# Which engine empties one transposed tile: two pairs of the first batch on VectorE instead of ScalarE, in a fused attention and MLP kernel

## The chip, the cores and the metric

The kernel runs on one core of a Trainium2 chip (trn2). The metric is the device time of one execution in microseconds, taken as the median over runs; the times quoted from a profile come from one profiled execution of the same program. Engines are named as in the profile: PE is TensorE (PEld its weight loads), DVE is VectorE, ACT is ScalarE, POOL is GpSimd, SP issues DMAs.

## What is computed

Inputs are fp32: four batches of eight heads, 576 positions, head size 64. Causal attention with a bias from a running sum is followed by two MLP blocks:

```python
scores = scale * np.matmul(q, k.transpose(0, 1, 3, 2))
cum = np.cumsum(np.maximum(s, 0.0), axis=-1)
bias = -(cum[:, :, :, None] - cum[:, :, None, :])
scores = np.where(causal, -1e9, scores + np.minimum(bias, 0.0))
attn = np.exp(scores - np.max(scores, axis=-1, keepdims=True))
attn = attn / (np.sum(attn, axis=-1, keepdims=True) + 1e-09)
x = np.matmul(attn, v)                       # heads side by side: 512 wide
h = gelu(x @ w_in); u, v = h[..., :512], h[..., 512:]
y = x + (u * (w_sg @ layernorm(v) + b_sg)) @ w_out
xk, xr = mixes of y and y shifted by one position
out = sigmoid(xr @ w_r) * (np.maximum(xk @ w_k, 0.0) ** 2 @ w_v)
```

## The kernel before

Each fp32 product is done as two or three products of parts: a value is cast to `F32R` (the high part) and the rest is kept as a low part (`split_lo`, L65). Weights of the first MLP come as 64-bit words and are put together by `convert` (L72 to L83): two ScalarE steps, two VectorE steps on `y` and `t` (L78, L80), a ScalarE cast (L83), a low part (L65).

`attn_pair` (L202 on) does two heads at a time. For each head, SP loads `kq`; the query half is cast into `qb` (L223, tile `QB`) and the key half into `ka` (L224); two DMAs (L225, L226) copy these parts to the other 64 partitions of `qa` and `ka`, and two splits on POOL (L65) write the low parts to `qa` and `kb` (tile `KB`). From the second batch on, and for most heads of the first, `QB` and `KB` are two fixed sets, used in turn, so the operands of a head can only be written when the head before the last is read for the last time. In the first batch heads go through three sets (`hd % 3`).

Nine score steps follow for a pair, by head and tile of 128 query rows: four of the first head, one (`2_4`) for the last 64 rows of both heads, four of the second head. A step multiplies the operands into a PSUM bank `sc` (L246, L247; two buffers), VectorE adds the mask and takes the row minimum of the negated scores (L271, `mx`), ScalarE takes the exponential (L279). Then PE transposes the tile in 128x128 blocks into a bank `tp` (L294, L297) and one copy takes the bank to SBUF: tile 1 to `pt1` by ScalarE (L299), tiles 2 and 3 to `pt2` (L301), the last 64 rows by two ScalarE copies and one of VectorE (L307, L308). Tile 3 is the one with four blocks, 128x512. In the first batch its copy was ScalarE's, in the others VectorE's. Its bank is one of the three `acc` banks in the first batch. In the end PE multiplies with the values (`pv`, L327) and the result, times the reciprocal sums, goes to `xT` (L340, L341).

`moe1(b)` is the first MLP of a batch: products `v` and `u` (L356) with evacuation by a gelu on ScalarE (L473), layer norm, `sg`, `o`. It is interleaved with the attention of the next batch. In the first batch all its PSUM banks are the three `acc` banks in turn. Its remaining weight pieces are loaded and converted on the way (`first_wc`, through three `tmp` buffers for `wr` and `wy`).

The program fixes the order in which instructions are created; a scheduler then sets the order on each engine from its own estimates of durations, so a changed engine for one copy can move instructions on all queues. Names in the order lists below carry a running number: `sc_2_4_1_782` is a score bank of step `2_4` (second chunk) of pair 3, and `tp_0_3_769` the transposes of tile 3 of the first head of pair 3. Pairs count from 0; pair 3 has heads 6 and 7, pair 4 heads 8 and 9.

Of the kernel before, what the change touches and what calls it, by code (L numbers as in the profile page):

```python
# [36 lines left out]
def fused_kernel(ctx, tc, kqT, vL, s, w_in, g_ln, w_sgT, b_sg, w_out, mu_k, mu_r, w_k, w_v, w_r, out):  # L37
    nc = tc.nc
# [163 lines left out]
    def attn_pair(b, hp):  # L202
        pr = b * (H // 2) + hp
        first = b == 0
        ops = []
        for hh in range(2):
# [5 lines left out]
            i = hd % (NSET + 1) if first else hd % NSET  # L212
# [31 lines left out]
        def scores(sc, hh, q, c0, c1, m):  # L244
            qa, ka, qb, kb = ops[hh]
            nc.tensor.matmul(sc[:m, :c1 - c0], qa[:, q], ka[:, c0:c1], start=True, stop=False)  # L246
            nc.tensor.matmul(sc[:m, :c1 - c0], qb[:, q], kb[:, c0:c1], start=False, stop=True)  # L247
# [3 lines left out]
        for hh, i in steps:  # L251
            q0 = i * P
            w = min(q0 + P, S)
            if first and hh != 1:
                st = stf[:, 64 * i * (i + 1):64 * (i + 1) * (i + 2)]
            else:
                st = at.tile([P, 640], F32, tag="st", name=f"st{pr}_{hh}_{i}", bufs=4)
            mx = at.tile([P, 2], F32, tag="mx", name=f"mx{pr}_{hh}_{i}", bufs=4)
            chunks = [(0, min(w, 512))] + ([(512, w)] if w > 512 else [])
            for ci, (c0, c1) in enumerate(chunks):  # L260
                sc = psum1.tile([P, 512], F32, tag="sc", name=f"sc{pr}_{hh}_{i}_{ci}", bufs=2)
                n = c1 - c0
                if hh < 2:
                    scores(sc, hh, slice(q0, w), c0, c1, P)
                    mk = mask[:, 512 - q0 + c0:512 - q0 + c0 + n]
                else:

                    scores(sc, 1, slice(w - P, w), c0, c1, P)
                    scores(sc, 0, slice(q0, w), c0, c1, 64)
                    mk = mask2 if ci else mask[:, :512]  # L270
                nc.vector.tensor_tensor_reduce(  # L271
                    out=st[:, c0:c1], in0=sc[:, :n], in1=mk, op0=ALU.add, op1=ALU.min,
                    scale=-SCALE, scalar=mx[:, 0:1] if ci else BIG, accum_out=mx[:, ci:ci + 1],
                )
            if hh == 2:

                nc.gpsimd.memset(st[:, w:w + 64], 0.0)
            last = len(chunks) - 1
            e = nc.scalar.activation(  # L279
                st[:, :w], st[:, :w], AF.Exp, bias=mx[:, last:last + 1], scale=-1.0,  # L280
                accum_out=sm[:, 4 * hh + i % 4:4 * hh + i % 4 + 1],
            )
            if gelus:
                after(e, gelus[-1])
            exps.append(e)
            yield 2 * w

            if i == 0:
                st0 = st
                continue  # L290
            tag = "acc" if first and i > 2 else "tp"
            tp = psum1.tile([P, 512], F32, tag=tag, name=f"tp{pr}_{hh}_{i}", bufs=3)
            if i == 1:
                nc.tensor.transpose(tp[:, 0:P], st0[:, 0:P], ident)  # L294
            for j in range(min(i + 1, 4)):
                c = (j + (i == 1)) * P
                nc.tensor.transpose(tp[:, c:c + P], st[:, j * P:(j + 1) * P], ident)  # L297
            if i == 1:
                nc.scalar.copy(pt1[:, hh], tp[:, :QS + P])  # L299
            elif i < 4:  # L300
                (nc.vector.tensor_copy if i == 3 and not first else nc.scalar.copy)(  # L301
                    pt2[:, hh, :i + 1, q0 - QS:w - QS], tp[:, :(i + 1) * P].rearrange("p (j m) -> p j m", m=P))
            else:
                tp4 = psum1.tile([P, 512], F32, tag="tp", name=f"tq{pr}", bufs=3)
                nc.tensor.transpose(tp4[:, 0:P], st[:, 512:640], ident)
                for a in range(2):
                    nc.scalar.copy(pt2[:, a, :4, q0 - QS:], tp.rearrange("p (j a m) -> p a j m", j=4, a=2)[:, a])  # L307
                nc.vector.tensor_copy(pt2[:, :, 3, 0:64], tp4[:, :P].rearrange("p (a m) -> p a m", a=2))  # L308
            yield (i + 1) * 200
# [6 lines left out]
        for r in range(2):  # L316
# [16 lines left out]
            for j in range(2):  # L333
                i = 2 * r + j
# [133 lines left out]
    def after(late, early):  # L468
        tc.add_manual_dep(late.ins, early.ins.name, mybir.DependencyInfo(mybir.DependencyClass.NoSync, mybir.DependencyReason.DATA),
                          reason="activation tables")  # L470
# [18 lines left out]


    pairs = [attn_pair(b, h) for b in range(B) for h in range(H // 2)]

    def a_stream():
# [173 lines left out]
```

## Time and profile before

| what | us |
|---|---|
| median of 3 runs | 719.56 (716.68 to 719.63) |
| profiled execution | 719.3 |
| its span, first to last instruction | 717.5 |
| PE busy | 675.9 (94%) |
| DVE busy | 405.7 (57%) |
| ACT busy | 386.6 (54%) |
| POOL busy | 243.5 (34%) |

The span is what the profile's instructions cover; the execution's own time is 1.8 us longer. Busy shares are means over stages: the first batch's attention fills about the first 85 us, attention and first MLP together go on to about 390, and the second MLP fills the rest.

### The profile page before, as it was taken

How to read it: one execution, taken by the hardware profiler on the slowest of the kernel's cores; microseconds unless marked ns; L12 is line 12 of the kernel's file. 1: busy time of each engine (PE TensorE's matmuls, PEld its weight loads, DVE VectorE, ACT ScalarE, POOL GpSimd, SP SyncE). 2: the span in 40 equal slices, each digit the busy share in tenths (PEclk: the TensorE clock that was granted, in tenths of full speed). 3: DMA queues.
4: the chain of work that ended last, by engine and by line, in shares of the span. 5: the costliest groups of instructions: out<-in, count | busy, mean ns of one | idle time of the engine just before them, and what ended most of it. 6: DMA issues, size and time to landing. Idle time of an engine off the chain costs nothing.

```text
span 717.5 us, 12717 instructions
## 1 busy us (share of the span) xinstructions
PE 675.9 (94%) x4720; PEld 604.8 (84%) x4720; DVE 405.7 (57%) x874; ACT 386.6 (54%) x878; POOL 243.5 (34%) x243
## 2 busy tenths in 40 slices
PE   2779988899999999999999989999999999999998
PEld 1456777787888878889878889899999999999997
DVE  7886586757663555672554579889535144413411
ACT  5777665856565565455564576689535144512400
POOL 7445544375352765253651120001502030330000
PEclk9979999999999999999999999999999999999999
DMA  7753533434533235524123763652310120000001
GB/s 214 211 192 106 148 99 122 139 112 131 160 114 118 70 84 164 163 66 152 35 54 92 242 209 119 179 167 93 107 43 6 62 67 1 17 25 27 1 18 48
DMA packets 33036, 74.95 MB, mean 104 GB/s; under 512 B 4368, under 2 KB 8464, under 8 KB 32976
## 3 DMA queue, kind: packets, MB, share of 16 engines
q1 hardware_dynamic: 32976, 74.15, 34.4%
q8 instruction: 37, 0.61, 0.4%
q14 instruction: 23, 0.19, 0.1%
HBM read 50.84 MB, written 13.79 MB: 90 GB/s over the span
## 4 chain that ended last, share of the span: by engine, by line
PE 80%; DVE 10%; DMA 4%; issue 3%; ACT 2%; POOL 0%; SPq 0%; DVEq 0%; ACTq 0%; POOLq 0%
PE vo L356 14%; PE k L356 14%; PE pv L327 8%; PE r L356 7%; PE o L356 6%; PE sg L356 6%; PE v L356 6%; PE u L356 5%; PE tp L297 4%; PE sc L246 4%; PE sc L247 3%; DMA wr<-in_w_out_dram 1%; DMA wc<-wscr 1%; DVE lt L559 1%; DVE QB L223 1%
## 5 line engine op out<-in xcount | busy, mean ns | idle before, releaser
L356 PE MATMUL k<-xvn,wk 128*128 128x288 f32 x768 | 102.9, 295 | 0.5 <-DVE y L460 0.5
L356 PEld LDWEIGHTS k<-xvn,wk 128*128 128x128 f32 x768 | 102.2, 188 | 0.8 <-DVE y L460 0.8
L279 ACT ACTIVATE st<-st,mx 128x128 f32<-128x128 f32 (+4 forms) x124 | 72.0, 582 | 43.1 <-DVE mx L271 42.7
L246 PE MATMUL sc<-ka,qa 128*128 128x512 f32 (+4 forms) x180 | 63.8, 360 | 23.0 <-DMA ka<-ka 11.6
L271 DVE CUSTOM_DVE_ANT_0 st<-sc,mask 128x512 f32<-128x512 f32 (+3 forms) x124 | 61.2, 504 | 25.6 <-PE sc L247 19.9
L327 PE MATMUL pv<-pt,vf 128*64 128x320 f32 (+4 forms) x448 | 66.9, 371 | 1.2 <-ACT u L473 1.0
L356 PE MATMUL sg<-wsg,vn 128*128 128x288 f32 x448 | 66.6, 299 | 0.1
L246 PEld LDWEIGHTS sc<-ka,qa 128*128 128x128 f32 (+1 forms) x180 | 33.3, 185 | 37.9 <-DVE mx L271 16.3
L356 PEld LDWEIGHTS sg<-wsg,vn 128*128 128x128 f32 x448 | 60.7, 188 | 2.2 <-issue 1.0
L65 POOL TENSOR_TENSOR KB<-kq,ka 64x576 fp32r<-64x576 f32 x29 | 43.3, 1493 | 51.1 <-ACT ka L224 34.7
L65 POOL TENSOR_TENSOR xvn<-lt,xvn 128x576 fp32r<-128x576 f32 x12 | 19.6, 1642 | 114.1 <-ACT xvn L560 74.3
L618 DVE SCALAR_TENSOR_TENSOR o<-vo,sg 128x288 f32<-128x288 f32 x32 | 14.5, 455 | 77.2 <-PE vo L356 77.1
L247 PE MATMUL sc<-KB,QB 128*128 128x512 f32 (+3 forms) x180 | 57.4, 334 | 0.6 <-DMA KB<-crt 0.6
L327 PEld LDWEIGHTS pv<-pt,vf 128*64 128x64 f32 x448 | 36.2, 138 | 25.6 <-issue 7.8
L356 PE MATMUL vo<-kh,wvb 128*128 128x288 f32 x256 | 56.5, 295 | 0.0
L356 PE MATMUL vo<-kh,wva 128*128 128x288 f32 x256 | 56.1, 295 | 0.0
L587 ACT ACTIVATE lk<-k 128x288 f32<-128x288 f32 x64 | 26.1, 408 | 50.4 <-PE k L356 46.2
L356 PE MATMUL r<-xxs,wr 128*128 128x288 f32 x384 | 53.2, 295 | 0.0
L356 PEld LDWEIGHTS r<-xxs,wr 128*128 128x128 f32 x384 | 51.7, 188 | 0.0
L297 PE MATMUL tp<-ident,st 128*128 128x128 f32 x300 | 49.0, 281 | 2.5 <-ACT st L279 2.5
L356 PE MATMUL v<-wv,xs 128*128 128x512 f32 x192 | 50.4, 401 | 0.7 <-ACT v L473 0.5
L65 POOL TENSOR_TENSOR qa<-kq,QB 64x576 fp32r<-64x576 f32 x29 | 43.9, 1512 | 16.5 <-DVE QB L223 6.1
(166 smaller groups left out, 1521.2 us busy)
## 6 DMA issues: line engine op xcount, KB each, us to landing
wc<-wscr SPq DMA_DIRECT2D x24, 512.0 KB
kq<-in_kqT_dram SPq DMA_DIRECT2D x32, 288.0 KB
vf<-in_vL_dram SPq DMA_DIRECT2D x16, 320.0 KB
ydram<-y SPq DMA_DIRECT2D x16, 288.5 KB
yt<-ydram SPq DMA_DIRECT2D x16, 288.5 KB
out_dram<-o SPq DMA_DIRECT2D x16, 288.0 KB
qa<-QB SPq DMA_DIRECT2D x30, 144.0 KB
ka<-ka SPq DMA_DIRECT2D x30, 144.0 KB
```

The costliest lines, as they stand in the source:

```text
L65: eng.tensor_tensor(out=lo, in0=x, in1=f32(hi), op=ALU.subtract)
L223: (nc.scalar.copy if hd < 2 else nc.vector.tensor_copy)(qb[64:128], kq[64:128])
L246: nc.tensor.matmul(sc[:m, :c1 - c0], qa[:, q], ka[:, c0:c1], start=True, stop=False)
L247: nc.tensor.matmul(sc[:m, :c1 - c0], qb[:, q], kb[:, c0:c1], start=False, stop=True)
L271: nc.vector.tensor_tensor_reduce(out=st[:, c0:c1], in0=sc[:, :n], in1=mk, op0=ALU.add, op1=ALU.min, scale=-SCALE, scalar=mx[:, 0:1] if ci ...
L279: e = nc.scalar.activation(st[:, :w], st[:, :w], AF.Exp, bias=mx[:, last:last + 1], scale=-1.0, accum_out=sm[:, 4 * hh + i % 4:4 * hh + i ...
L297: nc.tensor.transpose(tp[:, c:c + P], st[:, j * P:(j + 1) * P], ident)
L327: nc.tensor.matmul(acc[64 * a:64 * a + 64, o:n], vf[:, a, kk], pt, start=(kk == 0), stop=(kk == nk - 1))
L356: nc.tensor.matmul(acc, a, w_, start=(i == 0), stop=(i == n - 1))
L559: nc.vector.scalar_tensor_tensor(out=t, in0=yt[:, 1:S + 1], scalar=mu[:, r, 0, k:k + 1], in1=t, op0=ALU.mult, op1=ALU.add)
L587: nc.scalar.activation(t[:, c], acc[:, :HF], AF.Relu, scale=1.0 / WS)
L618: nc.vector.scalar_tensor_tensor(out=o[:, c], in0=acc[:, :HF], scalar=1.0 / WS, in1=sg[m][:, c], op0=ALU.mult, op1=ALU.mult)
```

## The change

Line 301 picks the engine that copies tile 3's bank. Before, it was VectorE in all batches but the first. Now it is VectorE also in the first batch for `hp` 2 and 3, the third and fourth pair. Each pair has the copy twice, once per head, so four copies change engine.

```diff
-                (nc.vector.tensor_copy if i == 3 and not first else nc.scalar.copy)(
+                (nc.vector.tensor_copy if i == 3 and (not first or hp > 1) else nc.scalar.copy)(
                     pt2[:, hh, :i + 1, q0 - QS:w - QS], tp[:, :(i + 1) * P].rearrange("p (j m) -> p j m", m=P))
```

The scheduler's order changes on all five queues, from the first of these copies (about 57.5 us in the profile before) to the score steps of the third batch's third pair (about 259 us); behind that the orders agree. Three places:

PE, around the last score step of pair 3. Before, it stands ahead of the `pv` products of pair 2:

```order
L246 MATMUL sc_2_4_1_782<-ka_725,qa_724 128x64
L247 MATMUL sc_2_4_1_782<-KB_84,QB_82 128x64
L246 MATMUL sc_2_4_1_782<-ka_710,qa_709 64x64
L247 MATMUL sc_2_4_1_782<-KB_83,QB_81 64x64
L327 MATMUL pv_1_687<-pt_2_561,vf_547 64x320 x5
L327 MATMUL pv_1_687<-pt_2_561,vf_547 64x192 x2
```

With the change:

```order
L338 MATMUL rt_698<-ident,rc_672 64x64 x2
L294 MATMUL tp_0_1_747<-ident,st_f_734 128x128
L297 MATMUL tp_0_1_747<-ident,st_f_734 128x128 x2
L297 MATMUL tp_0_2_758<-ident,st_f_734 128x128 x3
L297 MATMUL tp_0_3_769<-ident,st_f_734 128x128 x4
L246 MATMUL sc_2_4_1_782<-ka_725,qa_724 128x64
L247 MATMUL sc_2_4_1_782<-KB_84,QB_82 128x64
L246 MATMUL sc_2_4_1_782<-ka_710,qa_709 64x64
L247 MATMUL sc_2_4_1_782<-KB_83,QB_81 64x64
L246 MATMUL sc_1_0_0_802<-ka_725,qa_724 128x128
```

The step has moved behind pair 2's `pv` and `rt` products and behind the transposes of pair 3's first head; `ka_710`, `qa_709`, `KB_83` and `QB_81` are head 6's operands, whose buffers head 8 (`ka_895`, `qa_894`) takes next.

DVE, where pair 5 begins (scores `1456` to `1510`), one piece of the difference:

```order
 L223 CAST QB_82<-kq_1442 64x576
+L65 TENSOR_TENSOR wsg_94<-wsr_1089,wsg_93 128x576
 L271 ISA st_0_0_1456,mx_0_0_1457<-sc_0_0_0_1458,mask 128x128
 L271 ISA mx_0_0_1457 128x1
-L65 TENSOR_TENSOR wsg_94<-wsr_1114,wsg_93 128x576
 L271 ISA st_0_1_1463,mx_0_1_1464<-sc_0_1_0_1465,mask 128x256
 L271 ISA mx_0_1_1464 128x1
+L65 TENSOR_TENSOR wsg_94<-wsr_1114,wsg_93 128x576
 L271 ISA st_0_2_1496,mx_0_2_1497<-sc_0_2_0_1498,mask 128x384
```

The fourth `wsg` split goes behind the reduction of the 256-column score, and the third comes down to stand ahead of the 128-column one.

ACT, in the first batch's MLP, from the evacuation of `u_1_0` on. Before:

```order
L473 ACTIVATE u_1_1213<-u_1_0_1214 128x288
L404 CAST vn_0_1041<-v_1037 64x512
L83 CAST wcs_1193<-wy_1_1204 128x256
L473 ACTIVATE u_1_1213<-u_1_1_1228 128x288
L72 ACTIVATE wy_0_1244<-wr_0_1243 128x256
L77 ACTIVATE wy_0_1244<-wr_0_1243,mhalf 128x256
L473 ACTIVATE u_2_1262<-u_2_0_1263 128x288
L83 CAST wcs_1242<-wy_0_1244 128x256
L473 ACTIVATE u_2_1262<-u_2_1_1277 128x288
L72 ACTIVATE wy_1_1253<-wr_1_1252 128x256
L77 ACTIVATE wy_1_1253<-wr_1_1252,mhalf 128x256
L473 ACTIVATE u_3_1311<-u_3_0_1312 128x288
```

With the change, from the evacuation of `u_1_1` on:

```order
L473 ACTIVATE u_1_1213<-u_1_1_1228 128x288
L224 CAST ka_1682<-kq_1677 64x576
L83 CAST wcs_1193<-wy_1_1204 128x256
L72 ACTIVATE wy_0_1244<-wr_0_1243 128x256
L77 ACTIVATE wy_0_1244<-wr_0_1243,mhalf 128x256
L404 CAST vn_0_1041<-v_1037 64x512
L473 ACTIVATE u_2_1262<-u_2_0_1263 128x288
L473 ACTIVATE u_2_1262<-u_2_1_1277 128x288
L83 CAST wcs_1242<-wy_0_1244 128x256
L473 ACTIVATE u_3_1311<-u_3_0_1312 128x288
L72 ACTIVATE wy_1_1253<-wr_1_1252 128x256
L77 ACTIVATE wy_1_1253<-wr_1_1252,mhalf 128x256
```

Both `u_1` evacuations come ahead of the cast of the weight piece `wy_1_1204`, and `u_3_0` comes ahead of the steps on `wr_1_1252`; the `ka` cast of head 12 (`ka_1682`) comes down behind `u_1_1`. On DVE the two steps on `wy_1_1204` go ahead of the cast of `QB_81` for the same head.

## Rows read from the trace of the kernel before

**Rows 1.** The page: its head, and busy time of each engine.
```profile
span 717.5 us, 12717 instructions
...
PE 675.9 (94%) x4720; PEld 604.8 (84%) x4720; DVE 405.7 (57%) x874; ACT 386.6 (54%) x878; POOL 243.5 (34%) x243
```

**Rows 2.** Busy us by stretch: PE, PEld, DVE, ACT, POOL; PEclk, DMA share, GB/s.
```profile
38.90:42.40 3.50, 0.80 (x6) 0.47 (x5) 3.50 (x5) 3.13 (x11) 2.29 (x2) 0.94 0.36 86
42.00:52.20 10.20, 8.43 (x30) 5.67 (x31) 7.18 (x21) 7.21 (x19) 4.52 (x4) 0.50 0.72 242
57.00:71.27 14.27, 13.09 (x98) 9.85 (x96) 8.55 (x32) 11.78 (x35) 8.33 (x7) 1.00 0.46 127
71.27:77.00 5.73, 5.37 (x36) 4.15 (x35) 3.98 (x18) 5.73 (x19) 3.56 (x3) 1.00 0.53 149
94.00:99.30 5.30, 3.15 (x19) 2.10 (x17) 5.12 (x13) 5.27 (x12) 3.22 (x2) 1.00 0.46 115
99.30:129.70 30.40, 26.97 (x187) 22.97 (x185) 20.42 (x39) 19.08 (x46) 13.47 (x18) 1.00 0.36 113
129.70:262.00 132.30, 129.59 (x891) 109.04 (x892) 79.93 (x212) 76.50 (x193) 68.07 (x68) 1.00 0.39 114
```

**Rows 3.** Groups by line and form, 55 to 101 us: L301 (busy, mean ns).
```profile
L301 DVE COPY pt<-tp 128x512 f32<-128x512 f32 x2 | 1.4, 682 | 0.1
...
L301 ACT COPY pt<-tp 128x512 f32<-128x512 f32 x4 | 2.4, 593 | 0.0
```

**Rows 4.** Timeline of PE, 57 to 126 us: start, duration, idle before.
```profile
58.85 0.39 PE L246 MATMUL sc<-ka_f,qa_f 128*128 128x256 f32 x1 [0.49 <-DVE mx L271]
...
98.34 0.50 PE L246 MATMUL sc<-ka,qa 128*128 128x512 f32 x1 [1.40 <-DVE mx L271]
...
117.68 3.46 PE L356 MATMUL u<-xs,wcs 128*128 128x288 f32 x24 [2.03 <-ACT u L473]
...
124.00 0.87 PE L327 MATMUL pv<-pt,vf 128*64 128x256 f32 x8 [1.02 <-ACT u L473]
...
128.26 0.55 PE L297 MATMUL tp<-ident,st 128*128 128x128 f32 x3 [0.16 <-ACT st L279]
```

**Rows 5.** Timeline of DVE, 57 to 59 us.
```profile
58.14 0.45 DVE L224 CAST ka<-kq 64x576 fp32r<-64x576 f32 x1 [0.42 <-issue]
```

**Rows 6.** Timeline of all engines, 67 to 74 us.
```profile
67.00 0.22 PE L247 MATMUL sc<-KB,QB 128*64 128x64 f32 x1
...
68.00 1.57 POOL L65 TENSOR_TENSOR KB<-kq,ka 64x576 fp32r<-64x576 f32 x1 [3.14 <-ACT ka L224]
...
69.65 1.41 POOL L65 TENSOR_TENSOR qa<-kq,QB 64x576 fp32r<-64x576 f32 x1
...
71.27 0.31 PE L246 MATMUL sc<-ka,qa 128*128 128x128 f32 x1
...
72.41 1.43 POOL L65 TENSOR_TENSOR xs<-xT,xs 128x576 fp32r<-128x576 f32 x1 [1.35 <-ACT xs L369]
...
73.57 0.30 PE L246 MATMUL sc<-ka,qa 128*128 128x128 f32 x1
```

**Rows 7.** Timeline of DVE, 94 to 98 us.
```profile
94.08 0.76 DVE L65 TENSOR_TENSOR wsg<-wsr,wsg 128x576 fp32r<-128x576 f32 x1 [0.84 <-ACT wsg L194]
...
96.18 1.76 DVE L65 TENSOR_TENSOR wsg<-wsr,wsg 128x576 fp32r<-128x576 f32 x1
97.87 0.41 DVE L271 CUSTOM_DVE_ANT_0 st<-sc,mask 128x256 f32<-128x256 f32 x1
```

**Rows 8.** The chain that ended last, 112 to 124 us: start, duration, what.
```profile
113.28 1.58 DVE QB L223
...
115.36 1.52 DVE wy L80
...
118.46 4.27 DMA wr<-in_w_out_dram
...
123.66 0.59 ACT u L473 x2
```

## The prediction

> **What bounds the kernel now.** I read the page's head first, then the table of stretches, then the idle rows of TensorE's timeline, then the chain of waits where those rows are long. The head gives a span of 717.5 us in which PE is busy 675.9, 94% [rows 1]: PE's order and its gaps are the time. The profiled execution took 719.3 us, 1.8 more than its span and 0.3 under the median of the runs shown, 719.56; all sums below are against 719.3. The table of stretches says where the gaps lie that the change can reach [rows 2]. Its first moved copy stands at about 57.5 us and the last moved row of PE's order is one of the 64-column scores near 259, so what is before 57 us and behind 262 keeps its order and, I assume, its time. Between them PE's idle time is stretch minus busy: 14.27 - 13.09 = 1.18 us up to 71.27, 0.36 up to 77, 2.15 between 94 and 99.3, 3.43 between 99.3 and 129.7, 2.71 from there to 262. The first rows of the same table show the worst thing that idleness did in this run: between 38.9 and 42.4 PE was busy 0.80 of 3.50 us, and from 42.0 to 52.2 its granted clock was 0.50, the lower of its two levels (1.2 GHz); in the later stretches of the table it was 1.00. That drop lies ahead of the change.
>
> The gaps have two kinds of owner [rows 4]. PE waits for VectorE's reduction of the scores (`mx`), since the scores have two PSUM buffers: 0.49 us at 58.85, 1.40 at 98.34. And it waits for ScalarE's evacuation of `u`: 2.03 at 117.68, 1.02 at 124.00. VectorE and ScalarE are busy 57% and 54% of the span [rows 1], so what counts is which instruction stands ahead of the one that PE needs.
>
> **The change, part by part.** (a) *The four copies.* Four 128x512 evacuations change engines. On ScalarE one took 593 ns, on VectorE 682 [rows 3]. ScalarE is relieved of 4 x 0.593 = 2.4 us, VectorE loads 4 x 0.682 = 2.7. Neither number reaches the end by itself, since PE does the same work; the changed engine costs also move instructions on all five queues, DMA issues on SP and splits on POOL included, and that has to be priced stretch by stretch. That nothing but the engine changes is ruled out by the order lists above.
>
> (b) *57 to 71.3.* The first copy stands on VectorE ahead of the `ka` cast and the reduction of `sc_2_4_1`, for which PE waits at 58.85. VectorE was idle 0.42 us ahead of that cast [rows 5]; the copy fills the gap and pushes the rest by 0.68 - 0.42 = 0.26 us, or by all 0.68 if the gap was no free time. I take **+0.3**, nearest to the idle time in the row; ends +0.26 and +0.68.
>
> (c) *71.3 to 77.* Pair 3's last score step (`sc_2_4_1_782`) moves on PE from before the `pv` products to behind the transposes of `tp_0_3_769`, the place that PE reached at about 71.3. It is the last reader of head 6's operands, and head 8's go into the same buffers. In the trace it ran at 67.00, and behind it followed the `ka` cast on ScalarE and POOL's two splits (68.00 for 1.57 us, 69.65 for 1.41) [rows 6]: ready at 71.06, 3.84 us after the score's end at 67.22, and PE used it at 73.57 with 2.5 to spare. Now the step ends at about 71.6 (71.3 and (b)); the two DMAs of the same head, which SP issues behind the `QB` and `ka` casts, start later with it. POOL has its 1.43 us `xs` split ahead of them (72.41 in the trace), so I price 71.6 + 3.84 + up to 1.1 = 75.4 to 76.5. PE has until then only the eight scores and six transposes that took 71.27 to 73.57, and five more transposes, at 5.37 / 36 = 0.15 us each for a matmul of that stretch [rows 2]: 2.3 + 0.75 = 3.05, to 74.6. The wait is 0.8 to 1.9; VectorE's copy of `tp_0_3_769` ahead of the reduction of `sc_2_4_1_782` (0.68) and exps that start late on ScalarE fall beside it and make the longer end likelier. I take **+1.9**; the ends are 0, if the splits come in time, and 2.3, if the stretch's own 0.36 stays too.
>
> (d) *94 to 99.3.* PE's 1.40 us wait ends when VectorE has reduced a 256-column score (97.87). Ahead of that stood one split of `wsg` of 1.76 us; the same operation took 0.76 at 94.08 [rows 7]. In the new order the split that was long comes behind that reduction and another one of the kind, until now further up, stands two places ahead of it. With the shorter row for it the wait loses **1.0**; ends 0 (it takes 1.76 there too) and -1.4 (the whole wait goes). The Trainium skill (SBUF — State Buffer, Who interferes with whom) has VectorE operations with two SBUF inputs, as this subtraction is, block fully against a GpSimd operation that reads SBUF, whichever comes second; the two durations agree with such a lock on one of them. By that rule the split in the new place could be the blocked one, and the sum below would be 1.0 higher, 718.5.
>
> (e) *99.3 to 129.7.* Here the chain of waits can be read link by link [rows 8]: VectorE's `QB` cast of 1.58 us, the shift of a weight word (`wy`, L80) of 1.52, the low half (L65), the DMA of the next weight piece, 4.27 us from 118.46, and at last ScalarE's two evacuations of `u` (123.66), behind which PE's `pv` goes on at 124.00. ScalarE stands in the chain because it is in order: it waits for that DMA with finished `u` banks queued behind. The new order breaks it twice. ScalarE evacuates both halves of `u_1` before it waits for the cast of the weight piece, so the 2.03 at 117.68 goes; and it evacuates `u_3_0`, whose bank `pv_0` takes, before it waits for the DMA. `u_3_1` still comes behind the DMA, but the two `wy` operations now precede the `QB` cast, so the DMA can be issued 1.5 us earlier or more. 2.03 + 1.02 and two waits of 0.16 make 3.4; part of it may return, as the exps still wait for `u_3_1`. I take **-3.0**; ends -3.4 and 0.
>
> (f) *129.7 to 262.* Gaps of 2.71 us in all, waits for `mx` at most. The new order takes weight conversions out from between the reductions, but also puts eight score matmuls in a row with no `sg` product between. I take **0**; ends -2.7 (all of it goes) and +2.7 (as much again).
>
> Sum: 0.3 + 1.9 - 1.0 - 3.0 + 0 = -1.8. **719.3 - 1.8 = 717.5 us.**
>
> **The rivals.** *The chain of (e) holds through another link.* ScalarE's `ka` cast of head 12 now stands ahead of the weight cast, and it waits for a score step that PE does only behind `u_1`; later evacuations queue behind it. It decides if the DMA is issued no earlier than 118.46. For it: the new wait is real. Against: PE comes to that step about as early as VectorE came to its casts at 113.28. Time: without (e), 719.3 + 0.3 + 1.9 - 1.0 = 720.5. Chance 0.2.
>
> *Head 8 is not late.* If PE finds the operands ready in (c), 717.5 - 1.9 = 715.6. For it: 2.5 us of slack in the trace. Against: the step moves by more than that, from 67.22 to 71.6. Chance 0.2.
>
> *TensorE's clock falls in (c).* The one way to the slower side. PE would be idle 0.36 + 1.9 = 2.3 of some 8 us there, in several pieces. If that brings the lower level again for a stretch like the 10.20 us of [rows 2], it costs up to half of it, 5.1: 717.5 + 5.1 = 722.6, slower than before by 3; it decides once the waits of (c) lie as close as those of 38.9 to 42.4. Against it: between 94 and 99.3 PE was idle 2.15 of 5.30 and kept 1.00. The Trainium skill (Perfetto Trace Analysis, Matmul Optimizations) wants matmuls back to back because the engine scales with its use; by that rule this case gains weight, and its result would be the 722.6. The two stretches of this trace stand one for it and one against. Chance 0.13.
>
> **How the numbers follow.** The forecast has 0.47. Half a percent is 3.6 us, about what a measurement of this kernel can tell from no change; that puts the bounds at 716.0 and 723.2. Faster: six tenths of the second rival and, for the low ends of (d) and (f), a fifth of the forecast: 0.12 + 0.10 = 0.22. Slower: about half of the clock's case, a fifth of the first rival with a bad (f), and a little of the forecast: 0.07 + 0.04 + 0.03 = 0.14. The rest, 0.64, is within. The range takes in the second rival at its own 715.6 with some of (f), and the first with the ends of (c) and (f), and leaves out a good part of the clock's case: 713.8 to 722.4.
>
> **What would show it.** In the new profile: the four 128x512 copies on VectorE at some 0.68 us and only the first two pairs' four left on ScalarE; PE's wait at 58.85 near 0.8; a first score of pair 4 (head 8) at 76 or later with PE idle ahead of it; the wait at 98.34 below 1; no `u` row of PE waiting for ScalarE and `pv` beginning near 122; PE's clock at 1.00 from 57 us on. I am wrong if the `u` waits stay, if head 8's scores come with no gap, or if the time differs by what happens behind 262 us.

## The result, and the profile after

The changed kernel takes 726.60 us (median of 4 runs, 726.06 to 729.46) beside 719.36 for the kernel before: 1.0123 times as long, 95% interval 1.0104 to 1.0141. Measured again twice beside the experiments, it came to 1.0166 (1.0142 to 1.0190) and 1.0132 (1.0109 to 1.0156). So it is slower by 1.2 to 1.7%, 7 to 11 us. The forecast was 717.5 and the range ended at 722.4.

The page's head and first line after, to be held against [rows 1]:

```profile
span 724.5 us, 12706 instructions
...
PE 681.7 (94%) x4720; PEld 607.9 (84%) x4720; DVE 411.2 (57%) x878; ACT 384.7 (53%) x874; POOL 244.6 (34%) x243
```

The span grew by 7.0 us, and PE is busy 5.8 us longer on the same products. But 3.3 of the 5.8 lie ahead of the first moved copy (39.4 us busy up to 58.05, against 36.1 up to 57.60), where PE is only 0.45 us late. To see where the rest is lost, I cut both spans at places of PE's order ahead of which nearly the same products lie (the `sc` 64-column score of pair 2; the `rt` transposes of pair 3; the fifth `v` product; the first and the third `sg` product). Columns: stretch, length, PE busy (instructions), granted clock, DMA share, GB/s. The kernel before:

```profile
57.60:83.60 26.00, 24.46 (x168) 1.00 0.47 127
83.60:102.14 18.54, 16.39 (x91) 1.00 0.48 145
102.14:120.98 18.84, 16.81 (x120) 1.00 0.30 92
120.98:129.68 8.70, 7.30 (x57) 1.00 0.46 160
129.68:717.50 587.82, 574.86 (x4103) 1.00 0.31 93
```

The changed kernel:

```profile
58.05:88.19 30.14, 25.57 (x168) 1.00 0.39 109
88.19:110.63 22.44, 18.79 (x91) 0.86 0.45 122
110.63:127.36 16.73, 16.73 (x120) 0.98 0.28 86
127.36:135.95 8.59, 7.10 (x56) 1.00 0.41 127
135.95:724.50 588.55, 574.10 (x4103) 1.00 0.31 94
```

Line by line: +4.1 us in the first stretch, of which 3.0 are idle time (1.54 to 4.57); +3.9 in the second, 1.5 idle (2.15 to 3.65) and 2.4 busy, at a clock of 0.86; -2.1 in the third, where the waits for `u` are gone; -0.1; and +0.7 behind. With the 0.45 at which the first stretch starts late, that is 7.0. Of the 6.6 us behind the first copy, 4.1 are idle time and 2.5 longer busy time. The prediction had +2.2 for the first stretch, -1.0 for the second, -3.0 for the third and fourth together, and 0 behind.

The idle rows of PE after (timeline: start, duration, operation, idle time before it and what ended it), beside [rows 4]:

```profile
59.64 0.39 PE L246 MATMUL sc<-ka_f,qa_f 128*128 128x256 f32 x1 [0.83 <-DVE mx L271]
61.36 0.44 PE L246 MATMUL sc<-ka_f,qa_f 128*128 128x384 f32 x1 [1.21 <-DVE mx L271]
...
73.69 0.39 PE L246 MATMUL sc<-ka,qa 128*128 128x256 f32 x1 [0.47 <-DVE mx L271]
75.65 0.44 PE L246 MATMUL sc<-ka,qa 128*128 128x384 f32 x1 [1.46 <-DVE mx L271]
...
78.42 0.30 PE L246 MATMUL sc<-ka,qa 128*128 128x128 f32 x1
...
101.39 0.45 PE L246 MATMUL sc<-ka,qa 128*128 128x384 f32 x1 [1.28 <-DVE mx L271]
...
103.44 0.66 PE L297 MATMUL tp<-ident,st 128*128 128x128 f32 x4 [0.96 <-ACT st L279]
105.34 5.49 PE L356 MATMUL v<-wv,xs 128*128 128x512 f32 x12 [1.25 <-ACT v L473]
```

The waits at 61.36 and 75.65 were 0.31 and 0.32 us in the kernel before, and between 101 and 105 us stand three of about 1 us, where it had one of 1.40 [rows 4]. The row at 78.42 is the first score of head 8: PE did not wait for it.

Why 61.36 and 75.65? VectorE's cast of `QB` stands in front of the reductions there, and it is long (timelines of VectorE and of GpSimd):

```profile
59.61 1.35 DVE L223 CAST QB<-kq 64x576 fp32r<-64x576 f32 x1
...
73.67 1.60 DVE L223 CAST QB<-kq 64x576 fp32r<-64x576 f32 x1
```

```profile
59.07 1.58 POOL L65 TENSOR_TENSOR xs<-xT,xs 128x576 fp32r<-128x576 f32 x1 [1.86 <-ACT xs L369]
...
73.54 1.40 POOL L65 TENSOR_TENSOR xs<-xT,xs 128x576 fp32r<-128x576 f32 x1 [7.07 <-ACT xs L369]
```

Both times GpSimd's split of `xs` had begun before the cast, and the cast ends 0.3 us behind the split. Of the eight casts of this form between 43 and 140 us in the kernel before, six took 0.46. This is the second theory, after the prediction's: **the new order sets VectorE's casts behind GpSimd operations that are already running.** The Trainium skill (SBUF — State Buffer, Who interferes with whom) says that copies and casts can take the port that VectorE shares with GpSimd, and that whoever comes first keeps it for a whole instruction; the trace agrees, with 0.46 against 1.35 and 1.60.

### The profile page after: what moved, and what is told of

Same layout as the page of the kernel before. It is cut to its first block, busy times and chain, and to the rows that moved or that the text cites. A ratio compares the mean times of both kernels' runs of the same rounds, so it can differ in the third digit from the quotient of the medians.

```text
span 724.5 us, 12706 instructions
## 1 busy us (share of the span) xinstructions
PE 681.7 (94%) x4720; PEld 607.9 (84%) x4720; DVE 411.2 (57%) x878; ACT 384.7 (53%) x874; POOL 244.6 (34%) x243
## 4 chain that ended last, share of the span: by engine, by line
PE 79%; DVE 8%; DMA 6%; ACT 4%; issue 2%; SPq 0%; DVEq 0%; ACTq 0%
PE k L356 14%; PE vo L356 14%; PE pv L327 7%; PE r L356 7%; PE v L356 7%; PE o L356 6%; PE sg L356 6%; PE u L356 5%; PE tp L297 4%; PE sc L246 3%; PE sc L247 3%; ACT st L279 1%; DMA kq<-in_kqT_dram 1%; DVE QB L223 1%; DMA wr<-in_w_out_dram 1%
## 5 line engine op out<-in xcount | busy, mean ns | idle before, releaser
L246 PE MATMUL sc<-ka,qa 128*128 128x512 f32 (+3 forms) x180 | 64.3, 364 | 24.4 <-DVE mx L271 12.6
L246 PEld LDWEIGHTS sc<-ka,qa 128*128 128x128 f32 x180 | 33.4, 187 | 38.5 <-DVE mx L271 17.5
L356 PE MATMUL v<-wv,xs 128*128 128x512 f32 x192 | 52.4, 415 | 1.8 <-ACT v L473 1.8
```

The costliest lines, as they stand in the source:

```text
L356: nc.tensor.matmul(acc, a, w_, start=(i == 0), stop=(i == n - 1))
```

## The experiments

The scheduler's order can be held: a list of instructions, each tied to the one ahead of it on its queue when the schedule is made, with no wait added on the chip. So the engine of the copies and the order of everything else can be changed apart. In the diffs below, `ORDER` stands for that list.

### The copies, the order, and its two halves

Copies on VectorE with the order of before; copies on ScalarE with the order of the change; and the change with one half of the new order, cut near 95 us:

```diff
 e1_copies_only  copies: VectorE   ORDER = before
 e2_order_only   copies: ScalarE   ORDER = change
 e3_front_order  copies: VectorE   ORDER = change up to 95 us, then before
 e4_rear_order   copies: VectorE   ORDER = before up to 95 us, then change
```

> The four copies stand on VectorE as in the change, but every other instruction of all five queues is held in the order of the kernel before. Theory (the loss is made by the new order, not by the copies): 719.4 us like before, 718.5 to 720.5, since a copy of 0.68 us pushes a reduction in few places. Rival (VectorE is overloaded by the copies themselves, the order is innocent): 724 us or more, with PE's waits for the reductions as long as in the changed kernel, and the clock at its lower level near 110 us.

> The four copies stand on ScalarE as before, but every other instruction is held in the order of the changed kernel. Theory (order): about 726 us, 724 to 728, with PE's waits near 61, 75, 101 to 105 and 136 us and a stretch at the lower clock from about 105 us. Rival (copies): 720 us or less.

> The copies as in the change; the order of the changed kernel up to the place that PE reached at about 95 us (before the 256-column score of head 10), and behind it the order of before. Theory (each part of the new order has its own price, and the clock falls through the gaps of 94 to 106 alone): the idle time of 57 to 78 grew from 1.5 to 4.5 us, so 719.4 + 3.0 = 722.4 us, clock at its upper level near 105 us, and PE's waits for u are there again. Rival 1 (the gaps of the front already bring the clock down): 725 us or more. Rival 2 (the gaps of the front are made good later): 720 us or less.

> The copies as in the change; the order of before up to the place that PE reached at about 95 us, and behind it the order of the changed kernel. Theory: idle time +1.5 in 94 to 106, -3.4 where PE waited for u, +2 between 129 and 147, and 3.4 for half of a 6.8 us stretch at the lower clock: 722.9 us. Rival (the clock falls only when the gaps of the front precede, so it stays up here): 719.5 us.

| run | us | ratio to before (718.29) | 95% interval |
|---|---|---|---|
| copies only | 720.11 | 1.0026 | 1.0015 to 1.0037 |
| order only | 724.29 | 1.0083 | 1.0067 to 1.0098 |
| front order | 725.49 | 1.0095 | 1.0078 to 1.0113 |
| rear order | 719.41 | 1.0028 | 1.0013 to 1.0043 |

The order makes most of the loss, and it is the front half: with the copies it costs 0.95%, the rear half nothing beyond the copies (the rival's 719.5 came, not the 722.9). The copies cost 0.26%, 1.9 us, where (b) had 0.3. *Order only* is at the low end of its theory's 724 to 728, without the waits expected near 61 and 75 us. For the front order the number of rival 1 came, 725, but not its mechanism: the clock stayed at 1.00 from 57 to 80 us. PE waited 2.83 us at 103.0 and 1.50 at 105.2 for reductions, behind a `QB` cast of 1.60 and a `wsg` split of 1.86 on VectorE, and the clock fell there, although the order on VectorE was that of before again. Copies and order apart make 1.09%, together 1.2 to 1.7; the times alone do not show that they are more than additive, but VectorE's timelines show a loss that neither has alone. In *copies only* the two casts took 0.46 us, and in *order only* too, where no copy has pushed them behind the start of a split:

```profile
59.15 0.46 DVE L223 CAST QB<-kq 64x576 fp32r<-64x576 f32 x1
...
71.96 0.46 DVE L223 CAST QB<-kq 64x576 fp32r<-64x576 f32 x1
```

### GpSimd's order alone

The change, with two `xs` splits moved behind the splits of heads 7 and 8 on GpSimd:

```diff
+L65 KB1<-kq7,ka7
 L65 xs1<-xT1,xs0
-L65 KB1<-kq7,ka7
 ...
-L65 xs1<-xT2,xs0
 L65 KB0<-kq8,ka8
 L65 qa8<-kq8,QB0
+L65 xs1<-xT2,xs0
```

> The changed kernel once more, its order written out, as the measure for the three beside it. Both theories: 1.0123 times the time of before, within 1.0104 to 1.0141.

> The changed kernel, with GpSimd's order alone altered in two places: the xs split that the new order had put ahead of the KB split of head 7, and the xs split that it had put ahead of the splits of head 8, each come behind them. Nothing else moves. Theory (VectorE's QB cast takes 1.35 and 1.60 us instead of 0.46 because one of these GpSimd subtractions is already running): both casts fall to about 0.46, PE's waits of 1.21 at 61.4 and 1.46 at 75.7 fall to 0.3 to 0.5, and the time falls by about 2 us, to a ratio of some 1.0095; with luck the stretch at the lower clock goes too, then 1.006. Rival (my prediction's: PE waits at 75.7 because the operands of head 8 are late): the waits stay, ratio 1.012.

724.84 us, ratio 1.0098 (1.0077 to 1.0120), against 729.58 and 1.0166 for the change beside it: 4.7 us less. (The change itself came out above its expected interval; against 1.0123 and 1.0132, its two other measurements, the gain is some 2 us, with intervals that overlap.) VectorE's casts, GpSimd's splits and PE's waits in that run:

```profile
59.21 0.46 DVE L223 CAST QB<-kq 64x576 fp32r<-64x576 f32 x1
...
72.36 0.46 DVE L223 CAST QB<-kq 64x576 fp32r<-64x576 f32 x1
```

```profile
59.21 1.73 POOL L65 TENSOR_TENSOR KB<-kq,ka 64x576 fp32r<-64x576 f32 x1 [2.40 <-DVE mx L271]
```

```profile
60.05 0.45 PE L246 MATMUL sc<-ka_f,qa_f 128*128 128x384 f32 x1 [0.32 <-DVE mx L271]
...
73.20 0.44 PE L246 MATMUL sc<-ka,qa 128*128 128x384 f32 x1 [0.32 <-DVE mx L271]
```

The theory's rows came as written: both casts 0.46, both waits 0.32. At 59.21 cast and split start together, and now the split is the long one, 1.73 beside the usual 1.42: either can pay. The waits fell by 2.0 us, and the first stretch, from the `sc` score of pair 2 to the `rt` transposes of pair 3, by 1.9, to 28.22 against 30.14 and the 26.00 of before:

```profile
57.64:85.86 28.22, 25.55 (x168) 1.00 0.42 116
```

So the long casts are shown to cost about half of that stretch's +4.1; the other 2.2 have no experiment of their own. The rest of the 4.7 fits the clock, by the estimate of the next section: the change beside this run had 0.93 from 57 to 80 us and 0.86 from 135 to 160, this run 1.00 and 0.93.

### The clock

The change, with twenty transposes repeated, ten in each of two gaps:

```diff
+            if pr == 4 and hh == 1 and i in (2, 3):
+                for j in range(10):
+                    j %= i + 1
+                    nc.tensor.transpose(tp[:, j * P:(j + 1) * P], st[:, j * P:(j + 1) * P], ident)
```

> The changed kernel, with 20 transposes done again (the same input into the same place): 10 in PE's gap at 101.4 and 10 in the one ahead of the v products at 105.3, about 1.1 us each and so inside the gaps of 1.28 and 1.25. Theory (the clock fell because PE was idle 3.65 us between 94 and 106): the clock stays at its upper level from 105 to 112 us, and half of the 6.8 us comes back: ratio 1.0123 - 0.0047 = 1.0075. Rival (the clock falls for another reason, as the long load of the whole stretch, or earlier gaps): the lower stretch stays, ratio 1.012 or more.

727.38 us, ratio 1.0138 (1.0112 to 1.0165), 2.2 us under the change beside it. The expected 1.0075 did not come, and the intervals overlap, so the time alone decides nothing. The clock says more. Stretch 100 to 112 us of the changed kernel, and of this one:

```profile
100.00:112.00 12.00, 8.51 (x26) 0.72 0.40 113
```

```profile
100.00:112.00 12.00, 10.76 (x63) 1.00 0.37 100
```

0.72 over 12 us means that the lower level (1.2 GHz) held for 2 x 0.28 x 12 = 6.7 us; half of that, 3.4, is its price there when PE has work throughout. In the profile of the change beside this run the clock of that stretch was 0.86, in the third one 0.72 again. With the gaps filled the drop did not come there, in the one profile taken. That speaks for the gaps as its cause.

But the lower level came in other places, and these differ between executions of the same kernel. Stretches 57 to 80 and 135 to 160 us of the changed kernel's first profile, of the change beside this run, and of this run:

```profile
57.00:80.00 23.00, 18.43 (x129) 1.00 0.36 97
135.00:160.00 25.00, 21.33 (x148) 1.00 0.47 146
```

```profile
57.00:80.00 23.00, 18.70 (x122) 0.93 0.34 92
135.00:160.00 25.00, 22.67 (x137) 0.86 0.44 137
```

```profile
57.00:80.00 23.00, 18.70 (x117) 0.93 0.33 91
135.00:160.00 25.00, 22.38 (x146) 0.93 0.42 129
```

By the same sum over all stretches from 57 to 160 us, an estimate, the lower level held for 6.4 us in the first profile, 13.8 in the second and 6.7 in this one. Their executions took 726.63, 730.26 and 726.49 us: half of the 7.4 us between the first two is 3.7, and they differ by 3.6. So the spread between the measurements of the change fits the clock, and what the filled gaps kept near 105 us was lost elsewhere. In this run PE also waited 1.46 us for `u` at 128.8.

### The stretch from 94 to 106

Two attempts. First the two instructions that stand ahead of what PE waits for, alone and with the two GpSimd moves:

```diff
 DVE
-L65 wsg1<-wsr2,wsg0
 ...
 L271 st5_0_1<-sc5_0_1
+L65 wsg1<-wsr2,wsg0
 ACT
 L194 wsg0<-wsr2
+L279 st4_1_3<-st4_1_3,mx4_1_3
 L224 ka11<-kq11
 ...
-L279 st4_1_3<-st4_1_3,mx4_1_3
```

> The changed kernel a third time, as the measure for the two beside it, since its two measurements so far lie apart (1.0123 and 1.0166 times before). Expected between them, 1.0145, with the lower clock somewhere between 100 and 112 us again.

> The changed kernel with two instructions moved near 100 us and nothing else: VectorE's third split of wsg behind the reductions of the 128- and 256-column scores of head 10, and ScalarE's exp of the 512-column score of head 9 ahead of the ka cast and the wsg cast that waits for a DMA. Theory (the gaps of 94 to 106 come from these two standing ahead of what PE waits for): PE's wait of 1.28 at 101.4 falls to about 0.3, the 0.96 behind it to 0.3 or less and the wait for v by some tenths, 2 us in all, and with them the stretch at the lower clock near 105 us goes: 2 to 4 us less than the changed kernel beside it. Rival (the weights' DMAs are late and would be waited for anyway): the same waits come back under another name, within 1 us of the changed kernel.

> The changed kernel with the two moves near 100 us and the two of GpSimd's splits near 60 and 74 us together. Theory: about 2 + 2 us of waits and most of the lower clock go, 5 to 8 us less than the changed kernel beside it, a ratio of 1.002 to 1.007 to before, which is near the kernel whose copies alone were moved (1.0026). Rival (the rest of the new order costs too): 1.009 or more.

726.76 us, 1.0116 (1.0095 to 1.0137), and 724.41, 1.0092 (1.0073 to 1.0110), beside 727.62 and 1.0132. For the two moves the rival held, less than 1 us. All four gave 3.2 us less than the change beside them, not the 5 to 8 expected, and their rival's 1.009 came. With the two moves PE's three gaps became one, for `v` (the row ends with the view, at 106 us):

```profile
104.25 2.20 PE L356 MATMUL v<-wv,xs 128*128 128x512 f32 x6 [2.96 <-ACT v L473]
```

So something ahead of ScalarE's evacuation of `v` was late as a whole. ScalarE's timeline of the changed kernel shows what it waits for:

```profile
95.39 0.68 ACT L194 CAST wsg<-wsr 128x576 fp32r<-128x576 f32 x1 [1.36 <-DMA wsr<-in_w_sgT_dram]
96.51 0.68 ACT L194 CAST wsg<-wsr 128x576 fp32r<-128x576 f32 x1 [0.44 <-DMA wsr<-in_w_sgT_dram]
...
103.40 1.28 ACT L473 ACT_TABLE_LOAD   x1
```

and SP's queue why, first before, then changed:

```profile
83.51 0.33 SPq L211 DMA_DIRECT2D kq<-in_kqT_dram  x1
83.90 7.63 SPq L190 DMA_DIRECT2D wsr<-in_w_sgT_dram  x4
```

```profile
85.16 0.33 SPq L233 DMA_DIRECT2D vf<-in_vL_dram  x1
88.85 0.47 SPq L226 DMA_DIRECT2D ka<-ka  x1
...
92.23 1.07 SPq L190 DMA_DIRECT2D wsr<-in_w_sgT_dram  x2
```

The weights' DMAs were issued from 83.90 on; now they stand behind four DMAs of head 10's operands, of which the first waits until 88.85, and start at 92.23. The second attempt moves the first two of them back ahead of those four, on SP alone, and with all other moves:

```diff
+L190 wsr0<-in_w_sgT
+L190 wsr1<-in_w_sgT
 L226 ka10<-ka10
 ...
 L225 qa10<-QB0
-L190 wsr0<-in_w_sgT
-L190 wsr1<-in_w_sgT
```

> The changed kernel with SP's queue alone altered: the DMAs of the first two rows of the spatial weights (wsr) come ahead of the four DMAs of head 10's operands, as in the kernel before, instead of behind them. Theory (the gaps of 94 to 106 come from these two DMAs, for which ScalarE waits 1.28 and 0.57 us in its order, and all that follows, up to the first evacuation of v, is late by that): the wsg casts start more than 1 us earlier, PE's idle time between 94 and 106 falls from about 3.6 to 2.5 us or less, and the time by 1 to 3 us against the changed kernel's 1.012 to 1.017. Rival (ScalarE is bound by something else there): the idle time stays at 3.5.

> All the moves so far together: GpSimd's two, the two near 100 us, and SP's. Theory: against the four moves (1.0092), PE's wait of 2.84 for v shrinks by 1.2 to 1.8 us, and with less than 2.5 us idle there the clock stays up near 105 us: a ratio of 1.004 to 1.006. Rival (the lower clock near 105 to 147 us comes back in another place for whatever gap is left): 1.008 or more.

On SP alone: 723.18 us, 1.0083 (1.0055 to 1.0111). PE's waits between 94 and 106, and the clock from 100 to 112:

```profile
101.11 0.44 PE L246 MATMUL sc<-ka,qa 128*128 128x384 f32 x1 [2.07 <-DVE mx L271]
...
103.11 3.02 PE L356 MATMUL v<-wv,xs 128*128 128x512 f32 x12 [0.49 <-ACT v L473]
```

```profile
100.00:112.00 12.00, 10.40 (x60) 1.00 0.43 117
```

The waits add to 2.56 us in place of 3.65, the clock stays up there, and the twelve `v` products take 3.02 us, which in the changed kernel's profile took 5.49. From the `rt` transposes of pair 3 (87.17) to the fifth `v` product (105.97) PE took 18.80 us: the kernel before took 18.54, the change 22.44. So, by these profiles, the place of two DMA issues made nearly all of that stretch's loss, the clock's part included. The kernel's ratio is 0.4 to 0.8% under that of the change, which was not run beside it; the interval is clear of one of the change's three and just overlaps the other two. All five moves together gave 724.13, 1.0074 (1.0050 to 1.0097): no better than this one alone, and above the 1.0026 of the copies. That lies between the theory's 1.004 to 1.006 and the rival's 1.008, and the profile has what the rival said: with one wait of 2.35 us for `v` near 101 the lower clock was back (0.89 between 94 and 110, 0.93 between 135 and 160). What brings it down there, and the 2.2 us that the first stretch still loses, are not settled.

### The `u` stretch alone

The kernel before, with the changed order only from the first `u` product to the last:

```diff
 copies: ScalarE   ORDER = before, from u_0_0 to u_3_1 as in the change, then before
```

> The kernel before (copies on ScalarE, its own order), with the order of the changed kernel only from the first u product to the last one, about 104 to 122 us. Theory (step (e) of the prediction was right by itself): the waits for u of 2.03 and 1.02 us go, 3 us less than before, ratio 0.9958, 0.995 to 0.997. Rival (the waits went in the changed kernel only since PE came later): they stay, ratio 1.000.

717.15 us beside 718.45, ratio 0.9988 (0.9972 to 1.0004). The waits did go, but others came behind them:

```profile
118.32 2.01 PE L356 MATMUL sg<-wsg,vn 128*128 128x288 f32 x14
...
121.93 2.27 PE L327 MATMUL pv<-pt,vf 128*64 128x320 f32 x20 [0.44 <-ACT u L473]
...
125.27 0.44 PE L297 MATMUL tp<-ident,st 128*128 128x128 f32 x2 [0.81 <-ACT st L279]
```

Of all the kernels run this is the only one not slower than before, and it can't be told from it.

## Why the prediction was wrong, step by step

**The bound** was right: PE's order and gaps are the time. PE's busy time was taken as fixed, and it was not: of the 6.6 us lost behind the first copy, 2.5 came as longer busy time, nearly all in the stretch with the clock at 0.86.

**(a)** The price of a copy was right, about 0.68 us, and so was that the order has to be priced: it costs 0.83%, the copies 0.26. The copies alone still cost 1.9 us, where (b) gave 0.3.

**(b)** The wait at 58.85 grew from 0.49 to 0.83: +0.34 for a forecast of +0.26 to +0.68. What was left out is the cast right behind it, priced as in the trace of before though its neighbour on GpSimd had changed: +0.9 us at 61.36.

**(c)** The number was right by luck; the cause was not. The waits between 71 and 78 went from 0.32 to 0.47 + 1.46 + 0.31, +1.9 as forecast, but head 8 was not late (78.42, no wait): what the second rival said of it was so. The wait is for `mx`, behind a cast of 1.60 us; GpSimd's order alone took 1.14 of it away. In *order only*, where that cast was short, head 8's first score did wait for GpSimd, at 76.84, for 0.28 us. The stretch from 57 to 84 us as a whole lost 4.1, not 2.2.

**(d)** failed, and it is the largest miss: -1.0 forecast, +3.9 measured (1.5 of it waits, 2.4 longer busy time at a clock of 0.86), 4.9 of the 8.8 us between the forecast of -1.8 and the span's +7.0. With -1.0 there the change would still be slower, by 2.1. The step looked at which split of `wsg` stands before which reduction, and took it that splits and casts would find their data. Their DMAs had moved behind head 10's on SP; with two of them back ahead on SP the stretch took 18.80 us, 0.3 above the kernel before. The move stood in SP's piece of the order. Step (c) had counted SP's DMAs for head 8, step (d) had not. The sentence on the Trainium skill in (d) was about the right port in the wrong place: the third split took 0.76 and the fourth 1.12 instead of 1.76, and what was blocked was the `QB` casts near 60 and 74 us.

**(e)** The two waits vanished in the changed kernel as forecast, and the stretch is 2.1 shorter, though part of it ran at the lower clock. By itself the new order of that stretch gave 1.3 us (the interval reaches from a gain of 2.0 to a loss of 0.3), not 3.0: 0.44 came back as a wait for `u`, and 0.81 as a wait for an exp, of the kind that the step named and did not price.

**(f)** +0.7 instead of 0 in the first profile, within its ends; there the clock was 1.00 between 135 and 160 us. In the two other profiles of the change it was 0.86 and 0.93, a price that the step put at nothing.

**The clock's rival** had the right kind of price, half of the time at the lower level (5.1 us there, 3.4 measured), and the right sign, but it stood outside the sum and hung on the waits of (c) alone. In the first profile the clock stayed at 1.00 from 57 to 80 us and fell behind the gaps of 94 to 106, 3.65 us in four pieces of at most 1.28; in the two others it fell in both places (0.93 from 57 to 80). Its chance of 0.13 came from a stretch with 2.15 us idle that had kept its clock; after (d) had been taken for a gain, no one asked what 3.6 would do there.

## What to carry to other kernels

Where a scheduler sets the order, one changed engine is a change to every queue: go through the difference on each queue, DMA issues and GpSimd included, and ask of every moved instruction which engine runs beside it and what now stands ahead of it. Do not price an instruction by its duration in the old trace when its neighbours change. And where PE is busy 94%, ask of each new gap whether it will take the clock down with it, since that price, up to 3.4 us for one stretch here, is above that of a gap. One profile does not tell where the clock falls: compare several executions.

## What the runs showed of the hardware

- A 64x576 cast from SBUF to SBUF on VectorE took 0.46 us, and 1.35 or 1.60 when a GpSimd subtraction of two SBUF tiles was already running, ending 0.3 us behind it; where the two started together, it was the subtraction that took 1.73 instead of 1.42.
- The clock fell behind four gaps of at most 1.28 us each, 3.65 in all, and did not behind 2.07 and 0.49. With all moves together it fell behind one gap of 2.35, with 0.32 ahead of it. Three profiles of the same program had it at the lower level in different places. No rule that fits all of these is shown here.
- The four copies alone cost 1.9 us (1.1 to 2.7). Only 0.34 of it has a row, the wait of 0.49 at 58.85 that became 0.83; in that profile PE was already 1.1 us late ahead of the first copy, and the rest is open.
